# Moving the stationary and moving operands of three products to other places in SBUF, 32 to 288 bytes from where they were

## The chip, the cores and the metric

The kernel runs on one core of one Trainium2 chip. The metric is the device time of one execution in microseconds (us); lower is better. A comparison is read with a bound of 2%: inside it two kernels count as equal.

## The reference, cut to what matters

Three blocks follow each other. The first mixes in the frequency domain: `X = rfft(x)`, a complex product of X with `w_r + i w_i`, a bias, a soft threshold, and `irfft`. The second is a gated layer that mixes along the sequence, the third a two-layer network with a squared ReLU:

```python
h = np.maximum(x @ w_in, 0.0)                       # 4 x 3072 x 256 times 256 x 1024
u, v = h[..., :512], h[..., 512:]
v_n = (v - mean(v)) / sqrt(var(v) + 1e-6)
v_s = einsum('ts,bsd->btd', w_spatial, v_n) + b_spatial    # 3072 x 3072
x = (u * v_s) @ w_out
...
h = x @ w2_in                                       # 256 x 2048
g = s * relu(h) ** 2 + b
out = g @ w2_out                                    # 2048 x 256
```

`w_spatial` as the program uses it is split in four blocks along each axis, and the four batches make the columns, so that the einsum is a product of 3072 x 3072 by 3072 x 2048.

## The kernel before, in words

All matmuls take operands of type float32r, which has fewer bits of mantissa than float32. To keep the precision, each operand is split in two: a high part (ScalarE casts the float32 value, `high`, L834) and a low part (VectorE subtracts the high part from the value, `low`, L838). Each product is then three matmuls (`PASSES`): high by high, high by low, low by high. A tile with both parts has `_hl` in its name.

The program has three stages, issued by hand in one order (`manual_schedule`).

**Attention** (the first 540 us): transforms as small products, in an interleaved order: `ps_z`, `ps_g`, `ps_m`, `ps_v`, `ps_y`, and `ps_vp` (the `v` half of the gated layer). The mixing of channels, `ps_m`, is 12 matmuls of 256 columns (L414) and one for the bias (L416) for each of two halves.

**Mixing** (540 to 1812 us): the product with `w_spatial` by two levels of Strassen's scheme, 7 outer by 7 inner products. Each inner product runs over 6 steps along its inner axis (`NS`); there are 294 steps. A step `n` has a term `a` of 128 x 768 and a term `b` of 128 x 512, both split into `a_hl` and `b_hl`. `multiply(n)` (L857) issues 24 matmuls: 4 row blocks `d` of `b` (the stationary operand, 128 columns), 3 passes, 2 halves `h` of `a` (the moving operand, 384 columns). `run()` orders a step so: the matmuls of step n, then the high parts of step n+2, the sums of step n+3, the low parts of step n+2. So `a_hl` and `b_hl` have three buffers each, and step n uses the buffers n modulo 3. At the end of a product the result is copied or added out of PSUM (`evacuate`, L874, L878). The outer sums are made from DRAM: two loads and an addition (`st_a`, `st_b`, L775), by the queue of SP, and some results go back by the queue of POOL.

**Output** (1812 us to the end): 24 blocks of 512 tokens. For a block: `ps_u` (L1032, 24 matmuls), the gate, `ps_o` (L1050, 24 matmuls), which makes `x_hl`; then eight steps k of `layer1` (L1069: 12 matmuls, stationary `w6` to `w13`, moving `x_hl`), the squared ReLU with its split into `q_hl`, and `layer2` two steps later (L1090: 12 matmuls, stationary `w14` to `w21`, moving `q_hl`). All these matmuls have 512 columns. `q_hl` has three buffers, used in turn. The weights `w2` to `w21` lie in SBUF for the whole stage; `w2` to `w5` are in the pool `wts`, `w6` to `w12` in `wts_mid`, `w13` to `w21` in `wts_late`, loaded by `weight(j)` (L963).

A pool lays its tiles one behind the other in the order of their first use, each rounded up to 32 bytes of a partition. Pools of the side `left` lie one behind the other from the bottom of SBUF, those of the side `right` from its top. Of the buffers that the change touches, every one has a size that is a multiple of 256 bytes in a partition: `a_hl` 6144, `b_hl` 4096, `x_hl` and `q_hl` 8192, `r` 4096, a weight chunk 4096, `g` 16384. Together with the pools' bases (a tile `gap` of 1856 bytes in the pool `lines` sets that of the right side) this puts all operands of the mixing and of the output stage at an address that leaves 128 when divided by 256. So the distance of a stationary operand from the moving one is zero modulo 256, in all of the 7056 matmuls of the mixing and the 5760 of the output stage's four products. The slices that one matmul reads start at multiples of 512 bytes within a buffer and change nothing of this. In the first stage it is otherwise: `w_hi` and `w_lo` (moving in `ps_m`) leave 128, `xh` and `xl` (stationary) leave 192, which is a distance of 64; `cg` and `t_h`, `t_l` (`ps_g`) both leave 128; in `ps_z` the moving `x_hl` leaves 128 and the two halves of the stationary `cf` leave 128 and 0. The row of sums over the weights, `ps_row` (L1105, 16 matmuls of 512 columns), has moving weights that leave 128 and a stationary `ones` of two columns that leaves 192.

Of the kernel before, what the change touches and what calls it, by code (L numbers as in the profile page):

```python
# [9 lines left out]
F32 = mybir.dt.float32  # L10
F32R = mybir.dt.float32r
# [17 lines left out]
TB = 512  # L29
# [6 lines left out]
def f(ap):  # L36
    return ap.bitcast(F32)
# [693 lines left out]
def mixing(tc, nc, ws, vn, md, sd, convert_half):  # L731
# [5 lines left out]
    ring = left("m_ring", 3)  # L737
# [63 lines left out]
    term, hl = {}, {}  # L801
# [28 lines left out]

    def high(kind, n):
        t = term[kind, n]
        s = hl[kind, n] = ring.tile([128, 2, t.shape[1]], F32R, tag=kind + "_hl", name=kind + "_hl", bufs=3)
        nc.scalar.copy(s[:, 0, :], t)  # L834

    def low(kind, n):
# [52 lines left out]
    def split_first():  # L889
        n = begun[0]  # L890
        begun[0] += 1
        sums(n)
        for kind in "ab":
            high(kind, n)
            low(kind, n)

    def run():
# [12 lines left out]
        for n in range(total):  # L910
            now[0] = n
            multiply(n)
            ends = n % NS == NS - 1
            if n + 2 < total:
                high("a", n + 2)
                high("b", n + 2)
            if n + 3 < total:
                sums(n + 3)
            if ends:
                evacuate(n, 0)  # L920
                evacuate(n, 1)
            if n + 2 < total:
                low("a", n + 2)
                low("b", n + 2)
                freed(n + 2)
            if ends:
                evacuate(n, 2)
                evacuate(n, 3)
            outer_sums(3)
            if conversion and (todo or n % 3 == 2):  # L930
                conversion.pop()()
            loads()
            if n >= 6 and not conversion and not added and not todo and n % 3 == 0:
                conversion = [x for x in [convert_half(stage)] if x]
# [11 lines left out]
def output(tc, nc, yd, md, chunks, cd, bs, s_in, b_in, out):  # L946
# [3 lines left out]
    late = left("o_late", 2)  # L950
# [5 lines left out]
    gap = lines.tile([128, 464], F32, name="gap")  # L956
# [5 lines left out]

    def weight(j):  # L963
        pool = wts_late if j >= 13 else wts_mid if j >= 6 else wts
        t = pool.tile([128, 2, 512], F32R, tag=f"w{j}", name=f"w{j}")
        (nc.gpsimd if j >= 13 else nc.sync).dma_start(out=f(t) if j < 13 else t, in_=cd[j])
        return t
# [88 lines left out]
    NP = FF2 // 256  # L1056
    sq_t, oacc = {}, {}

    def layer1(n, k):
        x = x_t[n]  # L1060
        ps = rot.tile([128, 2, 512], F32, tag="rot", name="ps_h")
        for e in range(2):
            ff = 2 * k + e
            c = 0
            for j in range(2):
                w = w2[(ff // 4) * 2 + j]
                o = (ff % 4) * 128
                for a, i in PASSES:
                    nc.tensor.matmul(ps[:, e, 0:TB], w[:, a, o:o + 128], x[:, i, j, :], start=c == 0, stop=c == 5)  # L1069
                    c += 1  # L1070
        r = late.tile([128, 2, TB], F32, tag="r", name="r")
        s = late.tile([128, 2, 2, TB], F32R, tag="q_hl", name="q_hl", bufs=3)
        nc.scalar.activation(r, ps, AF.Relu)  # L1073
        nc.vector.tensor_mul(r, r, r)  # L1074
        nc.scalar.copy(s[:, 0], r)  # L1075
        nc.vector.tensor_sub(s[:, 1], r, f(s)[:, 0])  # L1076
        sq_t[n, k] = s
# [40 lines left out]

    fetch(0)
    win = [weight(2 + k) for k in range(2)]  # L1120
    load_terms(0)
    wo = [weight(4 + k) for k in range(2)]
    w2 = [weight(6 + j) for j in range(16)]
    load_terms(1)
    fetch(1)
# [11 lines left out]
    for j in range(len(steps) + 2):  # L1137
        if j < len(steps):
            n, k = steps[j]
            layer1(n, k)  # L1140
            if n == 0 and k == NP - 3:
                row = column_sums()
            if n == 0 and k == NP - 2:
                b_times(row)
            if n + 1 < len(blocks):
                for _ in range({0: 1 + (n == 0), 1: 2, 2: 1, 3: 2, 4: 1}.get(k, 0)):
                    if sums:
                        sums.pop(0)()
                if k == 0:
                    split(n + 1)  # L1150
                if k in (4, 5):
                    u_product(n + 1, k - 4)
                if k == 5 and n + 2 < len(blocks):
                    load_terms(n + 2)
                    fetch(n + 2)
                if k == 6:
                    out_product(n + 1)
            if k == NP - 1 and n + 2 < len(blocks):
                sums = combine(n + 2)
                sums.pop(0)()  # L1160
        if j >= 2:
            layer2(*steps[j - 2])
# [65 lines left out]
```

## Time and profile before

| | us |
|---|---|
| median of 2 runs | 3148.65 (3147.42 to 3149.89) |
| the profiled execution | 3147.44 |
| its span, first to last instruction | 3145.6 |
| TensorE busy | 3040.7 (97%) |
| VectorE busy | 2279.3 (72%) |
| ScalarE busy | 1395.4 (44%) |
| GpSimd busy | 393.2 (13%) |
| mean granted TensorE clock | 0.988 of full speed |

The profiled execution lies 1.8 us above its span and 1.2 us under the median. Busy shares are means over three stages with different limits. Matmuls overlap in the record: one of 512 columns is shown with some 389 ns although the next begins 227 ns after it, so that a time per matmul is read from the distance of starts, or from a count in a window that is full, and not from the mean duration.

### The profile page before, as it was taken

The page shows a single profiled execution, that of the slowest core. Times are in us where ns is not written, and L with a number is a line of the kernel's source. Part 1 is how long each engine was busy: PE and PEld are TensorE (multiplying, and loading weights), DVE is VectorE, ACT ScalarE, POOL GpSimd, SP SyncE. Part 2 cuts the span into 40 slices and gives each one's busy share as a digit, 9 for nine tenths or more (in the row PEclk, how much of TensorE's full clock was granted, in tenths as well). Part 3 has the DMA queues.
Part 4 walks back from the last instruction along what each step waited for, and adds up shares of the span by engine and source line. Part 5 has one row for each costly group of instructions (what it writes and reads, how often), then busy time and mean ns, then how long its engine had stood idle before and what let it go on. Part 6 is the DMA issues. An engine that isn't in the chain of part 4 may idle for free.

```text
span 3145.6 us, 42088 instructions
## 1 busy us (share of the span) xinstructions
PE 3040.7 (97%) x16040; PEld 2745.0 (87%) x16040; DVE 2279.3 (72%) x3275; ACT 1395.4 (44%) x2068; POOL 393.2 (13%) x497
## 2 busy tenths in 40 slices
PE   6999997999999999999999989999999999999999
PEld 5889885999999999999999968888888888888887
DVE  5788998798878788888878766566565665655664
ACT  5777766433334333433434324434343434334343
POOL 2665544021001200000000000000000000000000
PEclk7999999999999999999999999999999999999999
DMA  8987768586456956467471441202111211202010
GB/s 243 282 290 245 234 217 288 185 330 265 167 182 225 355 204 234 144 212 266 142 260 34 170 172 43 88 31 74 57 61 44 84 34 56 75 31 101 31 37 14
DMA packets 217602, 488.02 MB, mean 155 GB/s; under 512 B 21748, under 2 KB 66616, under 8 KB 217400
## 3 DMA queue, kind: packets, MB, share of 16 engines
q1 hardware_dynamic: 184328, 353.51, 33.4%
q0 software_dynamic: 33072, 131.82, 11.4%
q8 instruction: 126, 2.06, 0.3%
q14 instruction: 76, 0.62, 0.1%
HBM read 322.72 MB, written 162.53 MB: 154 GB/s over the span
## 4 chain that ended last, share of the span: by engine, by line
PE 75%; DVE 14%; DMA 6%; ACT 2%; issue 2%; SPq 0%; POOL 0%; ACTq 0%; DVEq 0%
PE acc L857 28%; PE oacc L1090 16%; PE ps_h L1069 16%; PE ps_o L1050 4%; PE ps_u L1032 4%; PE ps_m L414 2%; PE ps_vp L579 2%; DMA st_a<-in_moe_w_spatial_dram 1%; DVE a_hl L838 1%; DVE kept L874 1%; DMA st_b<-vn 1%; DVE b_hl L838 1%; DMA st_b<-t 1%; DMA vd<-v_sb 1%; PE ps_g L367 1%
## 5 line engine op out<-in xcount | busy, mean ns | idle before, releaser
L857 PE MATMUL acc<-a_hl,b_hl 128*128 128x384 f32 x7056 | 1239.9, 336 | 31.0 <-DVE kept L874 12.6
L857 PEld LDWEIGHTS acc<-a_hl,b_hl 128*128 128x128 f32 x7056 | 1233.7, 189 | 37.1 <-ACT kept L878 11.4
L1069 PE MATMUL ps_h<-x_hl,w 128*128 128x512 f32 x2304 | 553.5, 389 | 1.9 <-ACT x_hl L1053 1.2
L1090 PE MATMUL oacc<-q_hl,w 128*128 128x512 f32 x2304 | 553.4, 389 | 0.5 <-DVE q_hl L1076 0.5
L1069 PEld LDWEIGHTS ps_h<-x_hl,w 128*128 128x128 f32 x2304 | 432.5, 188 | 92.3 <-ACT x_hl L1053 1.6
L1090 PEld LDWEIGHTS oacc<-q_hl,w 128*128 128x128 f32 x2304 | 432.5, 188 | 90.4 <-DVE q_hl L1076 0.9
L834 ACT CAST a_hl<-a 128x768 fp32r<-128x768 f32 x253 | 211.8, 837 | 521.3 <-PE acc L857 442.6
L1074 DVE TENSOR_TENSOR r<-r 128x1024 f32<-128x1024 f32 x192 | 235.0, 1224 | 216.6 <-ACT r L1073 215.9
L1076 DVE TENSOR_TENSOR q_hl<-r,q_hl 128x1024 fp32r<-128x1024 f32 x192 | 235.3, 1226 | 214.5 <-ACT q_hl L1075 214.5
L1073 ACT ACTIVATE r<-ps_h 128x1024 f32<-128x1024 f32 x192 | 197.3, 1027 | 329.7 <-PE ps_h L1069 329.7
L838 DVE TENSOR_TENSOR a_hl<-a,a_hl 128x768 fp32r<-128x768 f32 x253 | 241.4, 954 | 136.0 <-ACT a_hl L834 135.4
L1075 ACT CAST q_hl<-r 128x1024 fp32r<-128x1024 f32 x192 | 201.8, 1051 | 283.2 <-DVE r L1074 283.2
L838 DVE TENSOR_TENSOR b_hl<-b,b_hl 128x512 fp32r<-128x512 f32 x295 | 202.0, 685 | 0.0
L834 ACT CAST b_hl<-b 128x512 fp32r<-128x512 f32 x295 | 181.7, 616 | 0.0
L875 POOL DMA_DIRECT2D md<-kept x112 | 60.7, 542 | 827.8 <-DVE kept L874 823.4
L579 PE MATMUL ps_vp<-win,y_hl 128*128 128x512 f32 x576 | 149.7, 396 | 1.6 <-ACT y_hl L479 1.2
L1032 PE MATMUL ps_u<-y_hl,w 128*128 128x512 f32 x576 | 140.3, 393 | 2.0 <-DVE y_hl L1018 2.0
L1050 PE MATMUL ps_o<-g,w 128*128 128x512 f32 x576 | 135.6, 390 | 2.5 <-DVE g L1040 1.5
L1032 PEld LDWEIGHTS ps_u<-y_hl,w 128*128 128x128 f32 x576 | 109.1, 190 | 25.6 <-DVE y_hl L1018 2.3
L1050 PEld LDWEIGHTS ps_o<-g,w 128*128 128x128 f32 x576 | 107.9, 188 | 26.2 <-DVE g L1040 2.1
L874 DVE TENSOR_TENSOR kept<-acc,kept 128x768 f32<-128x768 f32 x112 | 102.9, 951 | 22.0 <-PE acc L857 21.0
L579 PEld LDWEIGHTS ps_vp<-win,y_hl 128*128 128x128 f32 x576 | 101.2, 189 | 20.2 <-ACT y_hl L479 1.6
(139 smaller groups left out, 3662.8 us busy)
## 6 DMA issues: line engine op xcount, KB each, us to landing
a<-in_moe_w_spatial_dram SPq DMA_DIRECT2D x144, 384.0 KB, 5.3
b<-vn SPq DMA_DIRECT2D x168, 256.0 KB, 5.6
md<-kept POOLq DMA_DIRECT2D x112, 384.0 KB, 5.1
m<-md SPq DMA_DIRECT2D x42, 1024.0 KB, 7.3
st_a<-in_moe_w_spatial_dram SPq DMA_DIRECT2D x72, 384.0 KB, 6.7
vn<-vr POOLq DMA_DIRECT2D x96, 256.0 KB, 4.0
s<-a POOLq DMA_DIRECT2D x48, 384.0 KB, 5.9
x_f<-in_x_dram SPq DMA_DIRECT2D x32, 384.0 KB, 6.5
```

Of the source, the lines that this page charges most:

```text
L579: nc.tensor.matmul(ps, y[:, a, k, o:o + 128], win[k][:, w, :], start=c == 0, stop=c == 5)
L834: nc.scalar.copy(s[:, 0, :], t)
L838: sub(s[:, 1, :], term.pop((kind, n)), f(s)[:, 0, :])
L857: nc.tensor.matmul(acc[d][:, h, 0:TH], b[:, m, d * 128:(d + 1) * 128], a[:, w, h * TH:(h + 1) * TH], start=fresh and i == 0 and c == 0, st ...
L1032: nc.tensor.matmul(ps[:, d, 0:TB], win[k][:, a, o:o + 128], y[:, w, k, :], start=c == 0, stop=c == 5)
L1050: nc.tensor.matmul(ps[:, h, 0:TB], wo[k // 2][:, a, o:o + 128], g[:, w, k, :], start=c == 0, stop=c == 11)
L1069: nc.tensor.matmul(ps[:, e, 0:TB], w[:, a, o:o + 128], x[:, i, j, :], start=c == 0, stop=c == 5)
L1073: nc.scalar.activation(r, ps, AF.Relu)
L1074: nc.vector.tensor_mul(r, r, r)
L1075: nc.scalar.copy(s[:, 0], r)
L1076: nc.vector.tensor_sub(s[:, 1], r, f(s)[:, 0])
L1090: nc.tensor.matmul(ps[:, h, 0:TB], w[:, a, o:o + 128], s[:, i, e, :], start=ff == 0 and c == 0, stop=ff == 2 * NP - 1 and c == 2)
```

## The change

It adds tiles that nothing reads or writes (`gap`), so that the tiles behind them move, and it gives some tiles a tag of their own so that a gap fits between them. No instruction is added or taken away, and no order changes.

```diff
 def high(kind, n):
     t = term[kind, n]
-    s = hl[kind, n] = ring.tile([128, 2, t.shape[1]], F32R, tag=kind + "_hl", name=kind + "_hl", bufs=3)
+    if kind == "b" and n < 3:
+        ring.tile([128, 16], F32, tag=f"gap{n}", name="gap", bufs=1)
+    tag, bufs = (f"b_hl{n % 3}", 1) if kind == "b" else ("a_hl", 3)
+    s = hl[kind, n] = ring.tile([128, 2, t.shape[1]], F32R, tag=tag, name=kind + "_hl", bufs=bufs)
     nc.scalar.copy(s[:, 0, :], t)
...
 def weight(j):
     pool = wts_late if j >= 13 else wts_mid if j >= 6 else wts
+    if j > 14:
+        pool.tile([128, 8], F32, tag=f"gap{j}", name="gap")
     t = pool.tile([128, 2, 512], F32R, tag=f"w{j}", name=f"w{j}")
...
 def layer1(n, k):
...
-    s = late.tile([128, 2, 2, TB], F32R, tag="q_hl", name="q_hl", bufs=3)
+    z = (n * NP + k) % 3
+    if n == 0 and 0 < k < 3:
+        late.tile([128, (32, 40)[k - 1]], F32, tag=f"gap{k}", name="gap", bufs=1)
+    s = late.tile([128, 2, 2, TB], F32R, tag=f"q_hl{z}", name="q_hl", bufs=1)
```

The gaps are 64 bytes (three times, one ahead of each `b_hl`), 32 bytes (seven times, one ahead of each of `w15` to `w21`), and 128 and 160 bytes (ahead of the second and the third `q_hl`).

## Rows read from the trace of the kernel before

**Rows 1.** The page: span; busy us (share) by engine; the chain by engine.

```profile
span 3145.6 us, 42088 instructions
PE 3040.7 (97%) x16040; PEld 2745.0 (87%) x16040; DVE 2279.3 (72%) x3275; ACT 1395.4 (44%) x2068; POOL 393.2 (13%) x497
...
PE 75%; DVE 14%; DMA 6%; ACT 2%; issue 2%; SPq 0%; POOL 0%; ACTq 0%; DVEq 0%
```

**Rows 2.** Groups of TensorE: xcount | busy us, mean ns | idle before, releasers.

```profile
L857 PE MATMUL acc<-a_hl,b_hl 128*128 128x384 f32 x7056 | 1239.9, 336 | 31.0 <-DVE kept L874 12.6 <-ACT kept L878 8.4 <-ACT vr L617 5.2
L1069 PE MATMUL ps_h<-x_hl,w 128*128 128x512 f32 x2304 | 553.5, 389 | 1.9 <-ACT x_hl L1053 1.2 <-DVE x_hl L1054 0.8
L1090 PE MATMUL oacc<-q_hl,w 128*128 128x512 f32 x2304 | 553.4, 389 | 0.5 <-DVE q_hl L1076 0.5
```

**Rows 3.** Chain of waits, 540 to 1830 us: shares by line, then its longest pieces.

```profile
by line: PE acc L857 67.8%; DMA st_a<-in_moe_w_spatial_dram 3.6%; DVE a_hl L838 3.0%; DVE kept L874 2.8%; DMA st_b<-vn 2.8%; DVE b_hl L838 2.5%; DMA st_b<-t 2.4%; issue 2.2%; DMA c_w<-in_moe_w_in_dram 1.5%; DVE b L822 1.3%; DVE b L820 1.3%;
...
685.87 12.23 DMA st_a<-in_moe_w_spatial_dram
...
1262.22 164.62 PE acc L857 x948
```

**Rows 4.** Windows: us, busy us (xcount) PE PEld DVE ACT POOL, PE clock, DMA.

```profile
560.00:660.00 100.00, 100.00 (x579) 100.00 (x578) 83.36 (x121) 41.88 (x62) 8.67 (x16) 1.00 0.64 221
2100.00:2200.00 100.00, 100.00 (x443) 82.84 (x442) 59.13 (x50) 40.88 (x41) 0.00 (x0) 1.00 0.17 58
```

**Rows 5.** Timeline behind waits: start, us to the last end, engine, line, xcount.

```profile
837.07 1.23 PE L857 MATMUL acc<-a_hl,b_hl 128*128 128x384 f32 x6
...
1826.35 2.25 PE L1050 MATMUL ps_o<-g,w 128*128 128x512 f32 x9
...
1869.50 1.55 PE L1105 MATMUL ps_row<-w,ones 128*2 128x512 f32 x6
```

**Rows 6.** Timeline of the first stage, single matmuls of 256 columns: start, us.

```profile
135.57 0.28 PE L414 MATMUL ps_m<-w_hi,xh 128*128 128x256 f32 x1
...
136.59 0.28 PE L416 MATMUL ps_m<-bias,rows 128*128 128x256 f32 x1
136.71 0.28 PE L414 MATMUL ps_m<-w_hi,xh 128*128 128x256 f32 x1
...
138.12 0.28 PE L416 MATMUL ps_m<-bias,rows 128*128 128x256 f32 x1
...
217.09 0.28 PE L367 MATMUL ps_g<-cg,t_l 128*128 128x256 f32 x1
...
217.93 0.86 PE L340 MATMUL ps_z<-x_hl,cf 96*96 96x512 f32 x3
```

**Rows 7.** Waits of TensorE: us in total, times, longest us.

```profile
PE ps_y L462 <- DVE y_sb L470: 17.2, 22, 1.5
PE acc L857 <- DVE kept L874: 12.6, 6, 5.5
...
PE ps_g L367 <- ACT t_h L295: 8.5, 1, 8.5
```

## The prediction

> **What bounds the kernel now.** I read the page first: TensorE is busy for 97% of the span and makes 75% of the chain [rows 1]. A change that adds no instruction can then move the time by what a matmul takes, or by a wait. The groups of TensorE name the matmuls at stake: 7056 in the mixing, 2304 in each of the two layers, with a few us of idle time before them [rows 2]. The mean durations there overlap and are no use, so I took windows without a gap. A matmul counts in a window that it touches, so 579 of them fill 100 us and one duration of 0.336: 173.3 ns each. 443 of 512 columns fill 100.389 us: 226.6 ns each [rows 4]. At 2.4 GHz, the level that the clock column of these windows shows, 384 columns are 160.0 ns and 512 are 213.3. Both kinds pay the same excess of 13.3 ns per matmul, and they pay it evenly. That excess is all that a new place in SBUF can change.
>
> It isn't the same everywhere. Behind a wait the next matmuls are further apart: (1.23 - 0.336)/5 = 178.8 ns in the mixing and (2.25 - 0.389)/8 = 232.6 ns in the output [rows 5]; only after some five matmuls of the one and nine of the other does the even spacing begin, which then holds until the next wait. I read this as a rhythm that the stream falls into, here where all operands lie at distance zero modulo 256 bytes. In the first stage there are other distances [rows 6]. `ps_g`, at distance zero, takes 0.84/7 = 120.0 ns for 256 columns (106.7 + 13.3, the same excess). `ps_m`, at a distance of 64, takes 1.02/9 = 113.3 ns in one half (excess 6.7) and 1.41/12 = 117.5 in the next, with the same tiles' places modulo 256: two rhythms, both faster than the one at distance zero. So the place of the stationary operand bears on the spacing, and the sign is the question.
>
> How much of the mixing sets the end? The chain between 540 and 1830 us gives matmuls 67.8%, 874.6 us of 1290, which is 5046 of the 7056 at 173.3 ns. The rest is loads for the outer sums and VectorE [rows 3], beside which TensorE has slack. A change of the spacing there counts by 0.715. In the output stage it counts fully: VectorE is busy for 59 of 100 us [rows 4].
>
> **The change part by part.** Gaps of 64 bytes put the three `b_hl` at distances of 64, 128 and 192 from `a_hl`, which stays. All the 24 matmuls of a step have one distance; the next step has another. In the output stage the seven gaps of 32 bytes and the 128 + 160 bytes move more than they name. `late` grows by 288 bytes, so that `w6` to `w12`, `y_hl` and `g` move by 32 modulo 256. `wts_late` grows by 224 at the top, so that `w2` to `w5`, `w13` and `w14` move down by 224, which is 32 modulo 256 as well. Hence `ps_u` and `ps_o` keep distance zero; `layer1` goes from zero to 32 with all its weights; `layer2` meets, with weights 32 apart and `q_hl` at 0, 128 and 32, each of the eight multiples of 32 equally often. Two rules follow for the rhythm: in the mixing the moving operand stays and the distance changes every 24 matmuls, in the layers both change every 12.
>
> Mixing, lower price: each of 294 steps has to find its rhythm anew and then pays the old excess. Five matmuls at 178.8 - 173.3 = 5.5 ns: 294 x 5 x 5.5 x 0.715 = 5.8 us. Upper price, no rhythm at all: 7056 x 5.5 x 0.715 = 27.7 us. I take the lower, since `ps_m` shows that a rhythm exists at a distance of 64 and is found within a few matmuls [rows 6].
>
> Layers, lower price: nine of twelve at 232.6 - 226.6 = 6.0 ns, 4608 x 0.75 x 6.0 = 20.7 us. Upper: all of them, 27.6 us. The nearest row is `ps_row`, the one place with 512 columns and a stationary operand at another distance: (1.55 - 0.389)/5 = 232.2 ns over six matmuls at full clock, no even spacing found [rows 5]. Its stationary operand has two columns only, which makes it a poor likeness, but I have no better one. By it: 4608 x 5.6 = 25.8 us.
>
> Everything else I cost at nothing. The gaps are neither written nor read. Three tags with one buffer each rotate as one tag with three does, so step n + 2 waits for step n - 1 as before. Copies and splits on ScalarE and VectorE keep their sizes, and in the mixing VectorE has 17 of 100 us free to cover a longer one [rows 4]. Loads are the same in number and size, on the same queues. A shifted pool may make the first tile of a stage wait for one more old tile: between nothing and the longest wait that TensorE has on another engine's single release, 8.5 us [rows 7]. I take nothing, as loads are issued ahead by two steps or a block, and keep some of it in the range.
>
> Sum: 5.8 + 25.8 = 31.6 us. The profiled execution has 3147.44, 1.8 above its span and 1.2 under the median, so 3179 on its footing and 3180 on the median's; I say 3179. With both upper prices it is 3147.4 + 27.7 + 27.6 = 3203.
>
> **The rivals.**
>
> *A rhythm with less excess.* The stationary columns no longer come in step with the moving ones, as in `ps_m`. For it: both rows of `ps_m` lie under the 120.0 ns of `ps_g` [rows 6]. Against it: with 256 columns the next load of weights may be what sets the pace, which it doesn't with 384 or 512, and `ps_row` is slower. It decides if the spacing in the mixing falls under 173.3 ns. Priced by the mean of the two rows (115.4, so 4.6 ns less) in the mixing alone: 7056 x 4.6 x 0.715 = 23.2 us, 3124. With 6.7 ns everywhere: 33.8 + 4608 x 6.7 = 30.9, so 3083, the far end. Chance 0.25, a quarter of it near the far end.
>
> *Nothing changes.* The even excess is a fixed cost of a matmul and the place of weights is no part of it. For it: it is the same 13.3 ns at 256, 384 and 512 columns [rows 4, 6]. Against it: `ps_m` beside `ps_g`, same columns and another spacing. Time: 3147 to 3149, also where the gaps were laid out otherwise than I work out. Chance 0.18. The Trainium skill says this in its page "SBUF — State Buffer", section "Who interferes with whom": TensorE has one read port for the moving operand and another for weights, and "PE and ACT never wait on anyone". By that rule the time would be this rival's; the 113.3, 117.5 and 120.0 ns of one size speak against its letter.
>
> *A distance that collides.* Some distances may be worse than any loss of rhythm; this is the rival with a slowdown above 2%. Its place is the middle `b_hl` at 128 and the multiples in `layer2`. The one row near it is `ps_z`, whose stationary halves lie at 0 and 128: three matmuls of 512 columns in 0.86 us, (0.86 - 0.389)/2 = 235.5 ns, 8.9 more than the even spacing [rows 6]. If all moved operands paid that: 7056 x 8.9 x 0.715 + 4608 x 8.9 = 44.9 + 41.0 = 86 us, 3233. It decides from 8.9 x 0.73 = 6.5 ns per matmul on, where 63 us are lost. Against it: `ps_z` has 96 rows and columns and stands between other shapes, where `ps_g` too is uneven. Chance 0.10.
>
> **How the numbers follow.** The forecast, a rhythm lost and found again, has 0.47 and lies between 3170 and 3203. It is the likeliest, because it needs only what the rows show behind waits and in `ps_row`. The rival with less excess has 0.25, nothing 0.18, the collision 0.10. The range goes from 3112, under the milder price of the first rival, to 3212; it leaves out the far end of that rival and most of the collision. Two per cent of 3148.65 is 63 us, about what a measurement of this kernel can tell from no change. Faster than 3086 is only the far end: 0.07. Slower than 3212 is the collision and a little of the forecast with a late wait: 0.12. Within: 0.81.
>
> **What would show it.** In the profile of the changed kernel, full windows of the mixing should hold between 560 and 579 matmuls in 100 us (here 579), with more in a window just because a wait is missing; the layers should hold 430 to 433 instead of 443, while `ps_u` and `ps_o` keep 226.6 ns once in rhythm. Taken one buffer at a time, the three kinds of steps of the mixing should differ if the distance matters at all. I am wrong if steps at 64, 128 and 192 are all even at 173.3 ns (nothing changes) or lower (less excess), or if the layers count more than 443. The step that I trust least is the one from `ps_row` to the layers: it carries 25.8 of the 31.6 us.

## The result and the profile after

The changed kernel takes 3184.16 us (median of 2 runs, 3183.78 to 3184.54) against 3148.65: a ratio of 1.0114, with a 95% interval of 1.0098 to 1.0131. It is slower by 35.5 us, which lies inside the bound of 2% and well outside the scatter of the runs.

The page of the changed kernel first, with the same parts as [rows 1]: span, busy time by engine, the chain by engine.

```profile
span 3182.0 us, 42087 instructions
PE 3079.1 (97%) x16040; PEld 2754.7 (87%) x16040; DVE 2279.5 (72%) x3275; ACT 1396.0 (44%) x2068; POOL 392.1 (12%) x497
...
PE 79%; DVE 11%; DMA 6%; ACT 2%; issue 2%; SPq 0%; ACTq 0%; DVEq 0%
```

TensorE is busy for 38.4 us longer, and the span is 36.4 us longer. VectorE, ScalarE and GpSimd stand within 1.1 us of where they stood: a copy, a sum or a split doesn't mind the new places. So the question is only which matmuls became longer. The groups of TensorE in the changed kernel answer it (busy us, mean ns | idle before):

```profile
L860 PE MATMUL acc<-a_hl,b_hl 128*128 128x384 f32 x7056 | 1246.6, 338 | 32.2 <-DVE kept L877 13.3 <-ACT kept L881 9.8 <-ACT vr L617 5.2
L1074 PE MATMUL ps_h<-x_hl,w 128*128 128x512 f32 x2304 | 569.2, 396 | 1.9 <-ACT x_hl L1058 1.2 <-DVE x_hl L1059 0.8
L1098 PE MATMUL oacc<-q_hl,w 128*128 128x512 f32 x2304 | 566.1, 394 | 0.2 <-DVE q_hl L1084 0.2
...
L1055 PE MATMUL ps_o<-g,w 128*128 128x512 f32 x576 | 139.0, 397 | 2.3 <-DVE g L1045 1.3 <-ACT g L1044 0.8 <-ACT r L1081 0.2
```

Against [rows 2] the mixing has 6.7 us more work and 1.2 us more idle time, `layer1` 15.7 us more work and `layer2` 12.7. Busy times overlap; measured from the start of each matmul to the start of the next, the mixing takes 7.9 us more, `layer1` 15.4, `layer2` 12.4, `ps_u` 0.4 and `ps_o` 3.2, together 39.3 us ("by starts" below). The mixing also began 2.9 us earlier, at 538.3 us, which is no effect of the change: kernels with the same first stage begin it anywhere from 538.3 to 541.2.

Of the 3.2 us of `ps_o`, 2.6 come from the clock. In its first block of the stage twelve spacings in a row are 427 ns. The windows of that place, before and then after:

```profile
1826.00:1832.00 6.00, 4.67 (x18) 3.30 (x18) 0.68 (x1) 1.01 (x1) 0.00 (x0) 1.00 1.10 394
1831.00:1837.00 6.00, 6.00 (x15) 4.70 (x16) 0.00 (x0) 0.00 (x0) 0.00 (x0) 0.53 1.11 396
```

The granted clock is 0.53 in the second and 1.00 in the first, that is, mostly the lower level of 1.2 GHz instead of 2.4. In both kernels TensorE comes out of waits of 0.57 to 0.78 us there. The new places are not the reason: the kernel with the mixing's part alone (below), whose output stage is untouched, has the same 427 ns (granted clock 0.61 from 1833 to 1839 us), and the one with the output's part alone has 227. So the earlier begin and the slower clock, neither an effect of the change, nearly cancel in the 36.4 us.

Windows of the changed kernel, with the columns of [rows 4]:

```profile
560.00:660.00 100.00, 100.00 (x574) 100.00 (x573) 83.73 (x121) 41.17 (x62) 9.71 (x18) 1.00 0.64 217
2100.00:2200.00 100.00, 100.00 (x433) 81.09 (x432) 60.44 (x52) 39.89 (x40) 0.00 (x0) 1.00 0.12 41
```

Both are full and at full clock, so they hold no new wait: 579 matmuls have become 574, and 443 have become 433. A finer cut shows where in the mixing. Three steps in a row of the changed kernel, at distances 64, 128 and 192 (timeline: start, us to the last end, engine, line, xcount):

```profile
596.43 4.35 PE L860 MATMUL acc<-a_hl,b_hl 128*128 128x384 f32 x24
...
600.62 4.39 PE L860 MATMUL acc<-a_hl,b_hl 128*128 128x384 f32 x24
...
604.85 4.33 PE L860 MATMUL acc<-a_hl,b_hl 128*128 128x384 f32 x24
```

With the last duration of 0.334 us taken off, the 23 spacings are 174.6, 176.3 and 173.7 ns each; in the kernel before the steps without a wait have 173.3. Over all steps without a wait the means are 174.6, 176.1 and 173.5. The spacing within a step isn't a slow start with an even rest. At 128 the starts are 175, 181, 176, 173, 175 ns apart, and so on around through the whole step; at 64 they go from 170 to 178, to the end of the step; at 192 all but the last are 173 to 174.

In the output stage, three blocks of 12 of the changed kernel:

```profile
2100.72 2.96 PE L1074 MATMUL ps_h<-x_hl,w 128*128 128x512 f32 x12
2103.52 2.91 PE L1037 MATMUL ps_u<-y_hl,w 128*128 128x512 f32 x12
2106.26 2.97 PE L1098 MATMUL oacc<-q_hl,w 128*128 128x512 f32 x12
2109.07 1.09 PE L1074 MATMUL ps_h<-x_hl,w 128*128 128x512 f32 x4
```

From start to start these are 2.80, 2.74 and 2.81 us; 12 matmuls of the even spacing before (226.6 ns) take 2.72.

### The profile page after: what moved, and what is told of

The parts are those of the page before. It is cut to its first block, busy times and chain, and to the rows that moved or that the text cites. A ratio compares the mean times of both kernels' runs of the same rounds, so it can differ in the third digit from the quotient of the medians.

```text
span 3182.0 us, 42087 instructions
## 1 busy us (share of the span) xinstructions
PE 3079.1 (97%) x16040; PEld 2754.7 (87%) x16040; DVE 2279.5 (72%) x3275; ACT 1396.0 (44%) x2068; POOL 392.1 (12%) x497
## 4 chain that ended last, share of the span: by engine, by line
PE 79%; DVE 11%; DMA 6%; ACT 2%; issue 2%; SPq 0%; ACTq 0%; DVEq 0%
PE acc L860 31%; PE oacc L1098 17%; PE ps_h L1074 16%; PE ps_o L1055 4%; PE ps_u L1037 4%; PE ps_m L414 3%; DMA st_a<-in_moe_w_spatial_dram 2%; PE ps_vp L579 1%; DMA st_b<-vn 1%; DMA st_b<-t 1%; DVE a_hl L841 1%; DVE kept L877 1%; PE ps_g L367 1%; DVE bn L592 1%; PE ps_z L340 1%
## 5 line engine op out<-in xcount | busy, mean ns | idle before, releaser
L860 PE MATMUL acc<-a_hl,b_hl 128*128 128x384 f32 x7056 | 1246.6, 338 | 32.2 <-DVE kept L877 13.3
L860 PEld LDWEIGHTS acc<-a_hl,b_hl 128*128 128x128 f32 x7056 | 1240.3, 189 | 38.4 <-ACT kept L881 12.8
L1074 PE MATMUL ps_h<-x_hl,w 128*128 128x512 f32 x2304 | 569.2, 396 | 1.9 <-ACT x_hl L1058 1.2
L1098 PE MATMUL oacc<-q_hl,w 128*128 128x512 f32 x2304 | 566.1, 394 | 0.2 <-DVE q_hl L1084 0.2
```

Source lines behind the costliest of these rows:

```text
L860: nc.tensor.matmul(acc[d][:, h, 0:TH], b[:, m, d * 128:(d + 1) * 128], a[:, w, h * TH:(h + 1) * TH], start=fresh and i == 0 and c == 0, st ...
L1098: nc.tensor.matmul(ps[:, h, 0:TB], w[:, a, o:o + 128], s[:, i, e, :], start=ff == 0 and c == 0, stop=ff == 2 * NP - 1 and c == 2)
```

## The experiments

**The theories.** The forecast said that only a change of the distance costs: the stream loses its rhythm, finds it again, and pays the old excess from there on (theory C in the expectations). The main rival that the steps above suggest is that every distance modulo 256 has a spacing of its own, paid as long as it lasts (theory D). Two more came up on the way: that one distance may have two rhythms (E), and that a change of place costs even where the distance stays (Q). All distances are worked out from the sizes and the order of the tiles; no view shows an address. All times below are compared with runs of the kernel before on the same chip: 3146.14 us for the first four, 3147.38 for the next four, 3153.67 for 160 and 96, 3149.1 for the last. Where no interval is given, both are one run; ten runs of the kernel before on one chip spread over 7.8 us.

**The two parts alone.** The first kernel has only the edit of `high`, the second only those of `weight` and `layer1`:

```diff
# e1_mix_only: this and nothing else
-        s = hl[kind, n] = ring.tile([128, 2, t.shape[1]], F32R, tag=kind + "_hl", name=kind + "_hl", bufs=3)
+        if kind == "b" and n < 3:
+            ring.tile([128, 16], F32, tag=f"gap{n}", name="gap", bufs=1)
+        tag, bufs = (f"b_hl{n % 3}", 1) if kind == "b" else ("a_hl", 3)
+        s = hl[kind, n] = ring.tile([128, 2, t.shape[1]], F32R, tag=tag, name=kind + "_hl", bufs=bufs)
# e2_out_only: these and nothing else
+        if j > 14:
+            pool.tile([128, 8], F32, tag=f"gap{j}", name="gap")
...
-        s = late.tile([128, 2, 2, TB], F32R, tag="q_hl", name="q_hl", bufs=3)
+        z = (n * NP + k) % 3
+        if n == 0 and 0 < k < 3:
+            late.tile([128, (32, 40)[k - 1]], F32, tag=f"gap{k}", name="gap", bufs=1)
+        s = late.tile([128, 2, 2, TB], F32R, tag=f"q_hl{z}", name="q_hl", bufs=1)
```

> Only the three gaps ahead of b_hl; the output stage is as before. Theory C (it is the change of distance from step to step that costs, the even spacing being found again each time): the mixing stage as in the changed kernel, 574 matmuls in 100 us, output 443; 3148.7 + 8 = 3157 us. Theory D (each distance has a spacing of its own, whatever came before): the same here. Rival: the two halves of the change act on each other through the order in which they start; then this one alone is not 8 us (it would be 0 or below) and the two parts do not add up.

> Only the gaps of the output stage; b_hl as before. Theories C and D: mixing 579 matmuls in 100 us, layers 433, ps_u and ps_o a little under before; 3148.7 + 31 = 3180 us (14.6 of layer 1, 11.6 of layer 2, 5 of ps_u and ps_o). Rival as above: the sum of the two parts differs from the 36 us of the whole.

The mixing's part alone: 3154.54 us, ratio 1.0027 (1.0015 to 1.0038). The output's part alone: 3174.85, ratio 1.0097 (1.0082 to 1.0113). That is 8.4 and 28.7 us, where 8 and 31 were forecast. The two excesses make 0.0124 against 0.0114 for the whole, so within their intervals the parts add up and neither covers the other. The windows of the first:

```profile
560.00:660.00 100.00, 100.00 (x575) 100.00 (x574) 83.36 (x120) 41.43 (x62) 9.40 (x18) 1.00 0.63 215
2100.00:2200.00 100.00, 100.00 (x443) 82.84 (x442) 60.54 (x51) 40.59 (x41) 0.00 (x0) 1.00 0.17 59
```

and of the second:

```profile
560.00:660.00 100.00, 100.00 (x579) 100.00 (x578) 83.52 (x121) 41.92 (x63) 9.60 (x18) 1.00 0.64 219
2100.00:2200.00 100.00, 100.00 (x434) 81.12 (x433) 57.75 (x49) 40.04 (x41) 0.00 (x0) 1.00 0.17 58
```

Each part moves the count of its own stage and leaves the other at 579 or 443. In the first, the means at 64, 128 and 192 are 174.6, 176.1 and 173.5 ns, the same as in the whole change. Its group shows the idle time ahead of these matmuls:

```profile
L860 PE MATMUL acc<-a_hl,b_hl 128*128 128x384 f32 x7056 | 1250.0, 339 | 30.6 <-DVE kept L877 11.3 <-ACT kept L881 9.4 <-ACT vr L617 5.2
```

It is 30.6 us, as against 31.0 [rows 2]. From this row alone nothing of the longer matmuls seems to be absorbed by waits; the lengths of the stage in all kernels say otherwise (see the mixing in the part on the prediction).

**One distance everywhere.** These kernels keep all buffers in their old order and shift whole groups, so that every stationary operand of the mixing and of the output stage lies at the same distance d from its moving operand, all the time. Here for 192; the others differ in the sizes of the gaps:

```diff
+        if kind == "b" and n == 0:
+            ring.tile([128, 48], F32, tag="gap", name="gap", bufs=1)
...
-    gap = lines.tile([128, 464], F32, name="gap")
+    gap = lines.tile([128, 416], F32, name="gap")
...
+    wts_mid.tile([128, 48], F32, name="gap_mid")
+    outs.tile([128, 16], F32, name="gap_out")
```

> One distance everywhere: all b_hl at 192 modulo 256 from a_hl, and in the output stage all stationary operands at 192 from all moving ones, which stay at one place. Theory C: nothing changes from block to block, so the even spacing of before comes back, 579 and 443 matmuls in 100 us, 3148 us. Theory D: mixing 579 (the steps at 192 of the changed kernel had 173.5 ns), but the 512-column matmuls keep the 229.9 to 231.6 ns that layer 2 had at 192, so 434 to 437 in 100 us and 5760 x 4 ns = 23 us: 3171 us.

> As the run at 192, with 32 in its place. Theory C: 579 and 443 matmuls in 100 us, 3148 us. Theory D: the 512-column matmuls at 232.5 ns as layer 1 of the changed kernel, 432 in 100 us, 5760 x 5.8 = 33 us; the mixing at 32 is not known, between 173.3 and 179 ns, so 3181 to 3210 us.

At 192: 3160.12 us, ratio 1.0048 (1.0034 to 1.0062). At 32: 3184.72, ratio 1.0121 (1.0108 to 1.0135). Windows of the kernel at 32:

```profile
1450.00:1550.00 100.00, 100.00 (x579) 100.00 (x578) 83.25 (x138) 42.77 (x65) 2.16 (x4) 1.00 0.41 141
2100.00:2200.00 100.00, 100.00 (x431) 80.49 (x430) 58.09 (x50) 39.88 (x40) 0.00 (x0) 1.00 0.16 58
```

and at 192:

```profile
1450.00:1550.00 100.00, 100.00 (x579) 100.00 (x578) 83.27 (x138) 42.71 (x65) 2.16 (x4) 1.00 0.43 146
2100.00:2200.00 100.00, 100.00 (x438) 82.05 (x438) 59.05 (x50) 40.14 (x41) 0.00 (x0) 1.00 0.17 58
```

This is where theory C falls. Nothing changes its distance in the kernel at 32, and it loses as much as the whole change: in the output the starts alternate between 231.7 and 235 ns, 233.3 on average, and 5760 matmuls at 6.66 ns more than 226.67 are 38.4 us, against 38.6 measured. Its mixing, with 384 columns at the same distance, is untouched (579). So a distance that holds has a spacing of its own, and 32 isn't the only one: at 192 the output has a cycle of 226, 229 and 232 ns (228.9) and the mixing again nothing. Theory D's own price for 192, 23 us from the spacings that `layer2` had there between other distances, was too high: 14.0 us were lost.

The changed kernel also says something on the 256. Its `w6` to `w12` lie 288 bytes further from `x_hl` than before, not 32, and inside a block of `layer1` the starts alternate between 231 and 235 ns as they do at 32.

The other distances, for the spacing alone, one run each:

> One distance of 64 everywhere. Theory D (each distance has its own spacing): mixing 174.6 ns as the steps at 64 of the changed kernel, 574 or 575 matmuls in 100 us; 512 columns at 231 to 234 ns, 430 to 434 in 100 us; 3174 to 3186 us. Theory E (a distance has two rhythms, and the one that was entered by chance stays): mixing even at 173.3 ns from some wait to the next and at 174.6 between others. Theory C (only changes of distance cost): 579 and 443, 3148 us.

> One distance of 128 everywhere. Theory D: mixing 176.1 ns, 569 or 570 matmuls in 100 us; 512 columns at 230.5 to 233 ns, 431 to 435 in 100 us; 14 us of the mixing and 25 of the output, 3187 us. Theory C: 3148 us.

> One distance of 224 everywhere, which no step of the mixing had. Theory D: 512 columns at 230 to 233 ns as layer 2 had there, 430 to 435 in 100 us; the mixing not known, between 173.3 and 176.1 ns. If the order of the two streams counts (192 is 64 before, 224 is 32 before), 224 and 32 differ: 32 gave 233.3 and 173.3. Total 3170 to 3200 us.

> One distance of 160 everywhere. Theory D2 (each distance has a cycle of spacings, and none that was tried beats zero at 512 columns): 430 to 439 matmuls in 100 us in the output, and in the mixing a mean of 173.3 to 176.7 ns (the steps at 160 between others had 176.7, as had those at 224, which alone have 173.3). 3160 to 3200 us. Rival: 160 or 96 is the distance with a lower excess, as the small products of the first stage have at 64 (443 or more in the output, over 579 in the mixing, under 3140 us); then it is the better version.

> One distance of 96 everywhere, the last that is open. Theory D2: 430 to 439 matmuls in 100 us in the output; 579 in the mixing (the steps at 96 between others had 173.6 ns and ended even). 3160 to 3200 us. Rival as for 160: over 443 or over 579, under 3140 us.

| d | 512 columns, ns | 384 columns, ns | time less the kernel before, us |
|---|---|---|---|
| 0 | 226.7 | 173.3 | 0 |
| 32 | 233.3 | 173.3 | 38.6 |
| 64 | 233.3 | 174.3 (steps of 173.3 and of 174.7) | 43.5 |
| 96 | 234.3 | 173.5 (of 173.3, few of 176.7) | 35.4 |
| 128 | 232.4 | 175.8 (of 175.6 and of 176.1) | 47.3 |
| 160 | 233.3 | 176.7 | 50.5 |
| 192 | 228.9 | 173.3 | 14.0 |
| 224 | 233.3 | 174.1 (of 173.3, a fifth of 176.5) | 44.0 |

(Means of the starts in stretches without a wait.) Three times lie above their forecast: 3190.83 at 64, where theory D had at most 3186, 3194.66 at 128, where it had 3187, and 3204.16 at 160, where it had at most 3200. The times for 96 and 160 are compared with a run of the kernel before that is the slowest of all on record, 3153.67 us, so the last column is likely too small there. The windows of the worst of them, 160:

```profile
1450.00:1550.00 100.00, 100.00 (x568) 100.00 (x567) 83.34 (x132) 42.76 (x65) 2.16 (x4) 1.00 0.48 170
2100.00:2200.00 100.00, 100.00 (x430) 80.47 (x429) 59.61 (x50) 37.24 (x38) 0.00 (x0) 1.00 0.11 37
```

No distance beats zero with either number of columns, so no faster version comes out of this; the kernel before has the best of the eight. And theory E holds at 64, where the same mixing at the same distance shows two counts:

```profile
560.00:660.00 100.00, 100.00 (x575) 100.00 (x574) 82.69 (x119) 41.89 (x62) 8.79 (x17) 1.00 0.64 219
1450.00:1550.00 100.00, 100.00 (x579) 100.00 (x578) 82.85 (x138) 42.73 (x65) 2.16 (x4) 1.00 0.43 149
```

It holds at 224 as well:

```profile
1450.00:1550.00 100.00, 100.00 (x579) 100.00 (x578) 83.26 (x138) 42.71 (x65) 2.16 (x4) 1.00 0.42 143
1640.00:1740.00 100.00, 100.00 (x568) 100.00 (x567) 80.70 (x136) 41.97 (x63) 1.09 (x2) 1.00 0.19 62
```

Of the 280 steps without a wait there, 62 have 176.5 ns, 41 of them in a row from 1616 to 1789 us; at 96 it is 16 of 279 steps, with 176.7. Nearly always the rhythm changes at a wait of TensorE and then holds to the next wait. What picks one of the two at a wait, no run here shows.

**Places without distance.** Here the output stage keeps distance zero in every matmul, but `q_hl` and `w14` to `w21` together lie 32 bytes further than `x_hl` and the other weights, so that both operands change place from one block of 12 to the next. The mixing has its three `b_hl` at 96, 160 and 224.

```diff
+        if kind == "b" and n < 3 and (24, 16, 16)[n]:
+            ring.tile([128, (24, 16, 16)[n]], F32, tag=f"gap{n}", name="gap", bufs=1)
...
-    gap = lines.tile([128, 464], F32, name="gap")
+    gap = lines.tile([128, 456], F32, name="gap")
...
+    wts_mid.tile([128, 56], F32, name="gap_mid")
...
+        if j == 14:
+            pool.tile([128, 8], F32, tag="gap14", name="gap")
...
+        if n == 0 and k == 0:
+            late.tile([128, 8], F32, tag="gapq", name="gap", bufs=1)
```

> Mixing: the three b_hl at 96, 160 and 224, distances that it hasn't had; by theory D three kinds of steps with three means between 173 and 179 ns. Output: distance zero in all products, but q_hl and w14 to w21 lie 32 bytes further modulo 256 than the operands of the other three products, so that both operands change places every 12 matmuls. Theory P (only the distance counts): 443 matmuls in 100 us, 226.7 ns. Theory Q (a change of place between blocks costs too, which would explain ps_u and ps_o at zero with 229.8 and 228.0 ns in the changed kernel): 434 to 440.

It took 3170.14 us, 22.8 more than the kernel before. Blocks of 12 in its output:

```profile
2099.66 2.91 PE L1076 MATMUL ps_h<-x_hl,w 128*128 128x512 f32 x12
2102.41 2.89 PE L1039 MATMUL ps_u<-y_hl,w 128*128 128x512 f32 x12
2105.14 2.92 PE L1099 MATMUL oacc<-q_hl,w 128*128 128x512 f32 x12
2107.89 2.45 PE L1076 MATMUL ps_h<-x_hl,w 128*128 128x512 f32 x10
```

From start to start: 2.75, 2.73, 2.75. Over all, a block of the layers takes 32 ns more than 2720, in its first seven or so spacings, which go from 223 to 236 ns, after which it is back at about 227. So theory Q holds in this one run, and the loss that I forecast does exist, at distance zero even: some 2.7 ns per matmul, half of what I gave it. In the mixing the means at 96, 160 and 224 are 173.6, 176.7 and 176.7 ns. All steps at 224 have the slower of the two rhythms that 224 shows alone. That the step at 160 just ahead of them sets it is likely, but not shown.

**The same distance at another place.** At last both operands are moved by 32 bytes, in the mixing and in the output:

```diff
+        if kind == "a" and n == 0:
+            ring.tile([128, 8], F32, tag="gap", name="gap", bufs=1)
...
-    gap = lines.tile([128, 464], F32, name="gap")
+    gap = lines.tile([128, 456], F32, name="gap")
...
+    late.tile([128, 8], F32, tag="gap", name="gap_late", bufs=1)
```

> Moving and stationary operands of the mixing and of the output both 32 bytes further modulo 256, at one place throughout, so that every distance is zero as before. If the distance between the two is what counts, 579 and 443 matmuls in 100 us, 3147 us within 6. If the place of the stationary operand by itself counts (it lies where the run with one distance of 32 had it), 579 and 431, 3186 us.

3148.17 us against 3149.1 for the kernel before, and its windows:

```profile
1450.00:1550.00 100.00, 100.00 (x578) 100.00 (x578) 83.29 (x138) 42.83 (x66) 2.16 (x4) 1.00 0.44 147
2100.00:2200.00 100.00, 100.00 (x442) 82.80 (x442) 59.66 (x50) 40.30 (x42) 0.00 (x0) 1.00 0.17 58
```

These are one matmul off 579 and 443, where the kernel at 32 has 431 in the output. For a move of 32 bytes, the only one tried, it counts where the two operands lie to each other, not where either lies.

**The sum by theory D.** With the table, the change can be worked out without its own trace. `layer1` at 32: 2304 x (233.3 - 226.7) = 15.2 us, measured 15.4 by starts. `layer2` at each of the eight distances equally often: the mean of the second column is 231.9, 2304 x 5.2 = 12.0, measured 12.4. Mixing at 64, 128 and 192: 2352 x (1.0 + 2.5 + 0) = 8.2, measured 7.9. Together 35.4 us, where the three have 35.7 by starts. For `places` the same kind of sum, from the means of its own steps, gives 29 us, 16 of them in the mixing, against 22.8 measured; in its trace the mixing stage is only 12.4 us longer, which is most of the difference and is taken up below.

## Why the prediction was right in its number and wrong in its mechanism

- **What bounds the kernel: right.** TensorE alone moved, and apart from the clock in one block of `ps_o` the excess over 160.0 and 213.3 ns was all that changed. The windows came out at 574 and 433, where the prediction had 560 to 579 and 430 to 433.
- **Layers, 25.8 us: the size right, the reason wrong.** By starts they lost 27.8. The step that failed is that each change of distance loses the rhythm and that no even spacing is found in between, by which all 4608 matmuls paid the 5.6 ns of `ps_row`. At a distance of 32 the matmuls have an even or alternating spacing of 233.3 ns for good, without any change (the kernel at 32), and in the changed kernel `layer1` has 232.8. The row that I trusted least, `ps_row` at 232.2 ns [rows 5], gave the right size: its weights and its `ones` lie 64 apart, and the kernel at 64 has 233.3. It may have shown the spacing of a distance, which I read as a rhythm not yet found, but that isn't shown: its eight spacings at full clock go from 228 to 235 ns, where the kernel at 64 has 233 and 234 throughout. The rows behind waits, 232.6 [rows 5], are of the same size, but there the distance is zero.
- **Mixing, 5.8 us: the factor right, the price too small and wrongly reasoned.** The lower price, five matmuls in each step, failed: at 64 and 128 the excess runs through the step (1.2 and 2.7 ns over 173.4), at 192 it is next to nothing (0.1). 2352 x (1.2 + 2.7 + 0.1) = 9.4 us, where 294 x 5 x 5.5 = 8.1. The factor of 0.715 held. An estimate from the thirteen traces: the excess of the mixing's matmuls over 173.3 ns, worked out from the steps without a wait, goes from 0 to 23.8 us, and for each us of it the stage, from its first start to its last, is 0.74 us longer (a straight line through all kernels, standard error 0.04). At 160 throughout, for instance, 23.8 us of excess made a stage of 1290.1 us, where 32 and 192, with no excess, have 1271.7 and 1272.8. The 7.9 us of the changed kernel and the 9.8 of the mixing alone are measured against a single trace with 1270.5 us, which is low among the kernels without excess. The idle time of TensorE doesn't show the part that was absorbed: it is 30.7 us at 160 and 31.0 before [rows 2]. It doesn't count the wider spacings behind a wait.
- **`ps_u` and `ps_o` at nothing: wrong by 1 us.** Their distance stays zero and their spacing returns to 226 or 227 ns, as forecast, but they begin out of rhythm behind a block at another distance, with two to six spacings of 228 to 236 ns. 12 matmuls of `ps_u` take 2725 to 2746 ns from start to start, where they took 2720. The other 2.6 us of `ps_o` are those at the lower clock.
- **Everything else at nothing: right.** No wait took the place of another: the three tags with one buffer each rotate like one with three (idle 32.2 and 30.6 against 31.0), and the busy times of the other engines stand still.
- **The rivals.** *Less excess* is found at none of the eight distances with 384 or 512 columns. `ps_m` is below `ps_g`, but that is a matter of 256 columns, and I had it as a sign for the rest. *Nothing changes* is what the mixing does at 32 and 192 when one distance holds, and in most of its steps at 96 and 224. The rule of the Trainium skill that stood with it ("SBUF — State Buffer", "Who interferes with whom") is about engines that hold each other up, and it calls the two read ports of TensorE independent. No run shows another engine, or a port, to be the cause; but with the same instructions and the same work on the other engines, TensorE took 226.7 to 234.3 ns as the distance of its two operands changed, which that rule gives no reason to expect. *A collision* had the right place in the mixing, 128, where it is 176.1 ns, a third of the price; at worst it is 176.7 (at 160) and 234.3 (at 96, in the output), where I had 182.2 and 235.5.
- **Chances.** Had I seen that a spacing can belong to a distance, a sum by `ps_row` would have come out alike in the layers. The forecast was near by luck, and another choice of gaps would have shown it: with 192 throughout, my mechanism gives next to nothing, and the run lost 14.0 us.

**Left open.** What makes the excess. The spacings that are even are whole multiples of 6.67 ns (173.3 is 26 of them, 226.7 is 34, 233.3 is 35, and in the first stage 113.3 is 17 and 120.0 is 18), which is 16 periods at 2.4 GHz, and the others are cycles around such values. Why 384 columns mind 64, 128 and 160, and at times 96 and 224, while 512 mind every distance but zero, and why 256 columns were faster at 64 than at zero [rows 6], no run here tells.

## What to carry to other kernels

Where TensorE is busy all the time, the place of the two operands to each other is a term of its own. Read the spacing of starts per tile and per pair of buffers; don't take it for a constant of the shape. Here none of the eight distances was better than zero modulo 256 bytes for 384 and 512 columns, and a layout that loses it (another pool size, another first tile) cost 0.5 to 1.6% without one line of work changed. And a row that doesn't fit (`ps_row` here) should be asked how its operands lie before it is read as something on its way back to normal. To judge how much of a slowdown of one engine arrives at the end, compare the length of the stage over several kernels: here 0.74 of it arrived, close to the matmuls' share of the chain, 0.715, while the idle time of the engine hardly moved.

## What was not expected of the hardware

- The spacing of matmuls of one form depends on the distance of the addresses of stationary and moving operand modulo 256 bytes, as far as the eight multiples of 32 show: 226.7 to 234.3 ns at 512 columns, 173.3 to 176.7 at 384.
- It comes in cycles that last as long as the stream does: 231.7 and 235 ns in turn at 32, three spacings (226, 229, 232) at 192, five at 128 in the mixing of the changed kernel. One distance can have two in the mixing (64: 173.3 and 174.7 ns; 224: 173.3 and 176.5), and which one holds changes nearly always at a wait.
- At distance zero, a move of both operands by 32 bytes from one block of 12 to the next cost 32 ns per block (`places`), while the same move throughout cost nothing (3148.17 us against 3149.1).
